# An attention block and a gelu MLP on one core: the second tile's hidden layer in seven half-products, two groups of weight sums exchanged, and a new order of slots

## The chip, the cores and the metric

The kernel runs on one core of one Trainium2 chip. The metric is device time in microseconds of one execution of the whole program. Besides the bare times there is one profiled execution of the kernel, whose trace gives the start and the duration of every instruction. TensorE is called PE, VectorE DVE, ScalarE ACT, GpSimd POOL; SP is the queue that issues almost all DMAs.

## What is computed

A recurrent attention block (RWKV-6 style, batch 4, 8 heads, 768 steps, head size 48), whose output is read as 3072 rows of 384, followed by an MLP with an exact gelu:

```python
for t in range(S):
    cur = einsum('bhd,bhe->bhde', u[None] * k[:, :, t], v[:, :, t])
    y[:, :, t] = einsum('bhd,bhde->bhe', r[:, :, t], state + cur)
    state = w[:, :, t, :, None] * state + einsum('bhd,bhe->bhde', k[:, :, t], v[:, :, t])
x = y.transpose(0, 2, 1, 3).reshape(3072, 384)
h = x @ w_in                      # 384 x 2048
g = 0.5 * h * (1.0 + erf(h / sqrt(2)))
out = g @ w_out                   # 2048 x 384
```

All of it is fp32; the two weights arrive as float64 and are converted on the chip, in sixteen pieces.

## The kernel before

**Tiles and loops.** The 3072 tokens are eight tiles of 384 (`T`), numbered 0 to 7. Loop x of the main loop (from `for x in range(NX)`, L1242) issues three things woven into each other: the MLP of tile x-1 (`mlp`, L916), the attention of tile x (`attention`, L369) from where the loop before left it, and the first steps of the attention of tile x+1. After loop 7 the MLP of tile 7 runs alone. Every engine executes its own instructions strictly in the order in which they are issued, so the weaving fixes, for PE, DVE, ACT and SP, who stands behind whom.

**The order.** It is written out by hand as strings, `PLAN[x]` (L39). Each letter takes one step of a generator: `.` the MLP, `s` the attention of tile x, `f` that of tile x+1, `l` a load of the next tile's r, k, w, v, `c` a step of the weight conversion (loop 1), `w` sums of weights, `x` sums of x. What a string leaves over is drained at the loop's end (all but `f`), and the `s` of the next loop begins where `f` stopped.

**The hidden layer, two ways.** For tile 0 and 1 h is computed plainly: for each of 16 blocks of 128 hidden units, three products with 384 columns (L1070), then gelu on ACT (L1073; for even tiles the last 128 columns apart, L1075). For tiles 2 to 7 `h_halves` (L949) cuts x and w_in into halves and computes a 2 x 2 block product with seven products instead of eight, in products of 192 columns (all at L945): for each q of four, `first` (4 matmul instructions), `second` (8), `third` (8), `fourth` (8), `fifth` (4), `sixth` (4), `seventh` (8), 44 in all. Each plain product is two instructions, too: 96 for a tile. PSUM of `first` is copied to a second bank (L988), `fifth` and `sixth` are copied into g (L1008, L1012), `third` and `seventh` into one of two `o_sb` buffers (L981), which DVE adds to g (L999, L1017).

**The sums that this needs.** `h_sums` (L886, eight steps) makes them of w_in: w(1,0) grows in place by w(1,1), three others go to `s_of`. `sums_of_x` (L907, five steps: t3, t1, t2, t4, l01) makes them of the tile's own x, when its attention is done. `homes` (L873) takes the buffers for both, from those of the conversions. The second layer does the same with `w_sums` (L854, eight steps) and `first_sum` (L863, two): its seven products are run by `product` (L1082) in two halves of 8 instructions (L1084). `of_alone` products (end of the MLP of an even tile, 32 instructions) handle its last 128 tokens; odd tiles end with five more products. For tile 0 the second layer is plain (16 steps, L1164), and its two results are copied by ACT (L1170).

**The attention of a tile** from 2 on runs, in this order: DVE products (`f` steps, L407 stt, L394, L427, L401, L435), a layout by ACT and DVE (L573 to L579), bursts of small products on PE with h=4 and h=16 (L604; three bursts each, in even tiles the last two of h=16 are together with the first), whose results DVE (h=4, L637) or ACT (h=16, L620) copies out and so frees the PSUM pair, two of which exist; DVE updates (L658 to L669); transposes on DVE and twelve small DMAs (L552, L547), ACT's `L711`, the products kv (L727), the chain of states on DVE (L742, 20 of them), the products `inside` (L768) into PSUM pairs that the chain must have freed, a DVE read of their last columns called fence (L780), and the products y (L813) onto the same PSUM, which wait for the fence; then copies and DMAs into xT (L836 to L843). Tile 1 has another first half: six levels of products d (L468), updates (L521), copies (L532, for h=16 and 32 on ACT, L529), and a PE transpose kt (L701) that ACT copies (L703).

**Loop 1 and 2 before.** In loop 1 the letter `w` stands for masks (four steps) and `w_sums`; in loop 2 for `first_sum` and `h_sums`. The conversions are finished in loop 1: ACT makes three passes for each piece (L349 to L352), DVE a shift (L361) and an add (L365).

```python
        fast = x > 1
        if fast:
            yield from h_halves()
```

Of the kernel before, what the change touches and what calls it, by code (L numbers as in the profile page):

```python
# [38 lines left out]
PLAN = {  # L39
    0: ".lls.....sslsc.lsslll.sl.sls..sl.lscsl..sss.lscs.lscs.s.clll.s..s.pcsss...wss..sccs.ffp",  # L40
    1: (
        ".cswc.ccc.cccss.lc.ccscs..cc.cs.cclwcsc.ccssc.c.cccsccc..ssccc.c.lcls.cc.ccsc.w.clwscclccc"
        ".c.swcw.ss.ccs.lcsc..cwcccslccslff..w..fw.wfs..f..flffffffww"
    ),
    2: (
        "...l...s..ws.swssswssss.sslsw...ssss.sssws.ll..ws.w..lw.sw.wl.sls.sls..lf.s....sf..f.f.xx."
        "fxl.x.x"
    ),
    3: (
        "l..sss..s.s..s.s....s...s.ssllss.sss.s.s.ss.l..lsss..ssslss.ss.s..s......s..ls.llssf.sf.sf"  # L50
        "lf.f.x.x..xxfffxf"
    ),
    4: (
        "...s...lsl......s.s....sss..ssss..s..ss..s..s...llssslss....sl.sss...s...sll.sl.s.sfs..fsf"
        ".ff..xl.x.xfffxffx"
    ),
    5: (
        ".l..........ls.ss...s.sslls.ssss..ss.sls...sss..sssssl.ss.s..s.......s.lssll.sfsf.f.s.ff.x"
        "..x.xxxl"
    ),  # L60
    6: (
        "sss.sls.....s......ls.s....s.sssssss..s.....s.ss....s.s.ssss.s.l.ss.l.ls.l...s.l.lslssf.s."
        ".ffs..lff.xx..xffxffx"
    ),
    7: "......s.s....s.s...s.ssssss...sss.ss...sss..ssss.s...ss...s...s.s.ss.s.s.s.x.x...xxx",
}


# [5 lines left out]
def kernel(  # L74
# [6 lines left out]
    w_out: bass.AP,  # L81
    out: bass.AP,
):

    nc = tc.nc  # L100
    NX = rkw.shape[0]
    NP = u.shape[1]
# [22 lines left out]
    def fewer_pairs():  # L125
        pairs_of_banks.close()
        pools["d"] = ctx.enter_context(tc.tile_pool(name="pe", bufs=2, space=PSUM))
        pools["u"] = ctx.enter_context(tc.tile_pool(name="pu", bufs=1, space=PSUM))
        for i in range(2):
            u = bank_u(i)  # L130
            nc.tensor.matmul(u, lhsT=zeros[:, 0:128], rhs=zeros, start=True, stop=True)
# [51 lines left out]
    def load(x, dma):  # L183

        if x >= NX:
            return
        loaded[x] = [None, None]
        for i in (0, 2, 1):
            t = bufs[x % 2 if i == 0 else 1]
            for j in range(3):  # L190
                a = i * ALL + j * ALL // 3
                dma.dma_start(out=t[:, a:a + ALL // 3], in_=rkw[x, :, a:a + ALL // 3])
                yield
        load_v(x, dma)
        yield
# [12 lines left out]
    def weight_in(i, gate=False):  # L208

        if i < len(pieces):  # L210
            dst, src = pieces[i]
            raws[i] = cv.tile([128, PIECE], I64, name="raw", bufs=AHEAD) if wide else None
            if wide:
                dst = raws[i].rearrange("p (a c) -> p a c", a=dst.shape[1])
            if not gate:
                nc.sync.dma_start(out=dst, in_=src)
                return
            for a in range(dst.shape[1]):
                if wide:
                    nc.vector.memset(dst[:, a].bitcast(U32)[:, 0:1], 0)  # L220
                nc.sync.dma_start(out=dst[:, a], in_=src[:, a])
                yield
# [84 lines left out]
    def make_quarter_masks():  # L307
        make_fine()
        yield
        for (h, a), m_q in m_qs.items():  # L310
            nc.vector.tensor_tensor(out=quarter[h][a], in0=s_qs[h][:, 0:m_q.shape[1]], in1=m_q, op=ALU.is_equal)
            yield
# [538 lines left out]
    def w_quarter(b, c, k):  # L851
        return w_out_sb[:, b * HF + k * FG:b * HF + (k + 1) * FG, c * HM:(c + 1) * HM]

    def w_sums():  # L854

        sums.extend(cv.tile([128, HF, HM], F32, name="t", tag="raw", bufs=AHEAD) for _ in range(3))
        for out_, x, y in ((0, (0, 1), (0, 0)), (1, (1, 1), (0, 1)), (0, (1, 1), 0), (2, (1, 0), 0)):
            for k in range(2):
                o = sums[out_][:, k * FG:(k + 1) * FG]
                nc.vector.tensor_sub(o, w_quarter(*x, k), sums[y][:, k * FG:(k + 1) * FG] if isinstance(y, int) else w_quarter(*y, k))  # L860
                yield

    def first_sum():  # L863
        for k in range(2):
            nc.vector.tensor_sub(w_quarter(0, 1, k), w_quarter(0, 1, k), w_quarter(0, 0, k))
            yield
# [6 lines left out]
    def homes():  # L873

        more = [cv.tile([128, PIECE], I64, name="s", tag="raw", bufs=AHEAD).bitcast(F32) for _ in range(2)]
        s3_sb.append(more[0][:, 0:HF * 128].rearrange("p (f c) -> p f c", f=HF))
        x_sums.extend(z[:, i * HT:(i + 1) * HT] for z in (more[0][:, HF * 128:], more[1][:, HF * 128:]) for i in range(2))
        spare = [cv.tile([128, PIECE], F32, name=name) for name in ("f", "f", "e", "e")]
        for i, name in enumerate(("s1", "s2")):
            s12_of[name] = [z[:, 0:FG * 128].rearrange("p (f c) -> p f c", f=FG) for z in spare[2 * i:2 * i + 2]]  # L880
        second = [more[1][:, i * WI:(i + 1) * WI] for i in range(HK)]
        third = [s_home[:, i * WI:(i + 1) * WI] for i in range(HK)]
        fourth = [z[:, FG * 128:] for z in spare]
        s_of.extend((second, third, fourth))

    def h_sums():  # L886

        def w(a, c, k):
            return w_in_sb[:, a * HK + k * 2:a * HK + k * 2 + 2, c, :]

        def pieces_of(i, k):
            return s_of[i - 2][2 * k:2 * k + 2]

        for k in range(2):
            for i in range(2):
                nc.vector.tensor_sub(pieces_of(3, k)[i], w(0, 0, k)[:, i], w(1, 0, k)[:, i])
            yield
            nc.vector.tensor_add(w(1, 0, k), w(1, 0, k), w(1, 1, k))
            yield
            for i in range(2):  # L900
                nc.vector.tensor_sub(pieces_of(2, k)[i], w(1, 0, k)[:, i], w(0, 0, k)[:, i])
            yield
            for i in range(2):
                nc.vector.tensor_sub(pieces_of(4, k)[i], w(0, 1, k)[:, i], pieces_of(2, k)[i])
            yield

    def sums_of_x(x):  # L907

        xT = xT_of[x]
        x00, x01, x10, x11, l0, l1 = (xT[:, c, b * HT:(b + 1) * HT] for c in range(3) for b in range(2))  # L910
        t2, t3, t4, l01 = x_sums
        for o, a, b in ((t3, x11, x01), (x01, x01, x00), (t2, x11, x01), (t4, x10, t2), (l01, l0, l1)):
            nc.vector.tensor_sub(o, a, b)  # L913
            yield

    def mlp(x):  # L916
# [142 lines left out]
            late[:] = [rest]  # L1059

        s1, s2, s3 = [], [], []
        fast = x > 1
        if fast:
            yield from h_halves()
        for n, group in enumerate(() if fast else (0, 2, 1, 3) if halves else range(4)):
# [156 lines left out]
    def prepare_apart():  # L1222
        for i in range(2, 2 + HALFWAY):
            prepare(i)
            yield

    def next_v():
        load_v(1, nc.sync)
        yield

    def warm():
        for _ in range(2):
            keep_warm(3, True)
            yield

    def masks_and_sums():
        yield from make_quarter_masks()
        yield from w_sums()

    pieces_of_w = weights()  # L1240
    slots = iter(())
    for x in range(NX):  # L1242
        if x == 2:
            homes()
        following = attention(x + 1, 0) if x + 1 < NX else iter(())
        if x == 0:
            streams = {
                ".": units[0], "s": units[1], "f": following, "c": pieces_of_w, "w": next_v(), "x": warm(),
                "p": prepare_apart(),
                "l": chain(weight_in(0, True), islice(second, 5), weight_in(1, True), second, weight_in(2, True)),  # L1250
            }
        else:
            streams = {
                ".": mlp(x - 1), "s": slots, "f": following,
                "l": load(x + 1, nc.sync),
                "x": sums_of_x(x) if x > 1 else iter(()),
                "w": masks_and_sums() if x == 1 else chain(first_sum(), h_sums()) if x == 2 else iter(()),
                "c": pieces_of_w if x == 1 else iter(()),
            }
        for c in PLAN[x]:  # L1260
            next(streams[c], None)
        for c in ".slxwp" if x == 0 else ".slxwc":
            while next(streams[c], streams) is not streams:
                pass
        slots = following
        if x == 1:
            fewer_pairs()
    for _ in mlp(NX - 1):
        pass
# [60 lines left out]
```

## Time and profile before

| what | us |
|---|---|
| median of 3 runs (lowest, highest) | 594.47 (593.58, 595.18) |
| span of the profiled execution, first to last instruction | 595.7 |
| PE busy in it | 578.9 (97%) |
| DVE, ACT busy | 440.2 (74%), 280.9 (47%) |
| first product of the MLP of tile 0, 1, 2 | 48.85, 124.43, 197.12 |
| of tile 3, 4, 5, 6, 7 | 261.28, 332.47, 396.74, 467.93, 532.42 |
| last product of all begins | 592.4 |

Times of instructions are counted from the start of the span. A line of a timeline gives the start, the time from the first start to the last end, engine, line, operation, output and inputs with shapes, and how many; in brackets the idle time of the engine before it and what ended it. PE's instructions overlap: sixteen products of 192 columns follow one another every 162 ns, while each is shown with 326 ns, so gaps of PE under some 0.16 us do not show as idle, and the distance between starts is what counts.

### The profile page before, as it was taken

What the parts mean: (1) busy time and instruction counts of PE and PEld (TensorE: products, weight loads), DVE (VectorE), ACT (ScalarE), POOL (GpSimd) and SP (SyncE); (2) the same over time, 40 slices, a digit from 0 to 9 for tenths busy, and PEclk for the clock granted to TensorE, in tenths of its full rate; (3) what the DMA queues carried; (4) which work ended last, traced back from release to release, by engine and by line L of the source; (5) the groups of instructions that cost most, each with busy time, mean ns of one, the idle gap of its engine ahead of it and who ended that gap; (6) DMA issues with size and microseconds to landing.
All of it is one profiled execution on the core that took longest, in us unless ns stands there. A gap on an engine that the chain in (4) does not pass through costs nothing. (4 is left out here: it accounts for less than half of the span.)

```text
span 595.7 us, 17417 instructions
## 1 busy us (share of the span) xinstructions
PE 578.9 (97%) x7536; PEld 513.5 (86%) x7536; DVE 440.2 (74%) x854; ACT 280.9 (47%) x648; POOL 8.0 (1%) x21
## 2 busy tenths in 40 slices
PE   5789999999999999999999999999999999999998
PEld 3566666676799999999999999999999999999997
DVE  5868767888969987687859987688759998521332
ACT  2158889333622358045561458135560465435400
POOL 3100000000000000000000000000000000000000
PEclk9989999999999999999999999999999999999999
DMA  7657671120152211241023411330015200210000
GB/s 235 193 175 273 211 237 61 71 94 1 19 148 79 74 54 24 74 137 36 1 52 90 124 37 18 96 110 11 3 32 161 72 2 5 37 46 0 1 15 33
DMA packets 51004, 46.80 MB, mean 79 GB/s; under 512 B 31728, under 2 KB 36080, under 8 KB 50928
## 3 DMA queue, kind: packets, MB, share of 16 engines
q1 hardware_dynamic: 50832, 45.62, 25.5%
q8 instruction: 59, 0.97, 0.7%
q14 instruction: 17, 0.14, 0.1%
q10 hardware_dynamic: 96, 0.07, 0.1%
HBM read 36.24 MB, written 4.72 MB: 69 GB/s over the span
## 5 line engine op out<-in xcount | busy, mean ns | idle before, releaser
L945 PE MATMUL h_ps<-xT,w_in_sb 128*128 128x192 f32 x480 | 95.4, 330 | 0.5 <-DVE o_sb L1207 0.5
L945 PEld LDWEIGHTS h_ps<-xT,w_in_sb 128*128 128x128 f32 x480 | 79.7, 190 | 3.9 <-ACT g L977 1.5
L1070 PE MATMUL h_ps<-xT,w_in_sb 128*128 128x384 f32 x192 | 64.5, 491 | 0.9 <-ACT rkw L1075 0.9
L1070 PEld LDWEIGHTS h_ps<-xT,w_in_sb 128*128 128x128 f32 x192 | 35.7, 190 | 25.5 <-ACT rkw L1075 1.7
L1084 PE MATMUL o_ps<-w_out_sb,g 128*128 128x192 f32 x224 | 39.7, 326 | 0.0
L1084 PEld LDWEIGHTS o_ps<-w_out_sb,g 128*128 128x128 f32 x224 | 37.0, 190 | 0.3
L945 PE MATMUL u_ps<-s,w_in_sb 128*128 128x192 f32 x192 | 35.3, 327 | 0.0
L468 PEld LDWEIGHTS d<-rkw 64*64 64x64 f32 x1152 | 20.8, 147 | 16.7 <-issue 11.9
L620 ACT COPY a_sb<-d 32x256 f32<-32x256 f32 (+8 forms) x90 | 32.6, 362 | 4.6 <-PE d L604 3.1
L945 PEld LDWEIGHTS u_ps<-s,w_in_sb 128*128 128x128 f32 x192 | 31.8, 190 | 0.2
L1084 PE MATMUL o_ps<-w_out_sb,f 128*128 128x192 f32 x176 | 31.6, 329 | 0.0
L1084 PE MATMUL o_ps<-t,g 128*128 128x192 f32 x176 | 31.4, 329 | 0.0
L1084 PE MATMUL o_ps<-w_out_sb,e 128*128 128x192 f32 x176 | 31.4, 329 | 0.0
L1084 PE MATMUL o_ps<-t,e 128*128 128x192 f32 x176 | 31.2, 328 | 0.0
L1084 PE MATMUL o_ps<-t,s 128*128 128x192 f32 x176 | 30.9, 327 | 0.0
L468 PE MATMUL d<-rkw 64*64 64x64 f32 (+1 forms) x1152 | 23.5, 235 | 7.2 <-DMA rkw<-in_rkw_dram 4.1
L742 DVE SCALAR_TENSOR_TENSOR st<-st,tot_sb,kv_ps 128x48 f32<-128x48 f32 x160 | 29.0, 256 | 1.7 <-PE kv_ps L727 1.6
L637 DVE COPY_PREDICATED a_sb<-quarter,d 128x480 f32<-128x480 uint8 (+5 forms) x54 | 23.2, 438 | 8.6 <-PE d L604 7.3
L1084 PEld LDWEIGHTS o_ps<-t,g 128*128 128x128 f32 x176 | 28.7, 190 | 0.4
L1084 PEld LDWEIGHTS o_ps<-w_out_sb,e 128*128 128x128 f32 x176 | 28.7, 190 | 0.3
L1084 PEld LDWEIGHTS o_ps<-w_out_sb,f 128*128 128x128 f32 x176 | 28.7, 190 | 0.3
L1084 PEld LDWEIGHTS o_ps<-t,e 128*128 128x128 f32 x176 | 28.8, 190 | 0.2
(163 smaller groups left out, 1127.0 us busy)
## 6 DMA issues: line engine op xcount, KB each, us to landing
rkw<-in_rkw_dram SPq DMA_DIRECT2D x54, 256.0 KB, 4.0
raw<-in_w_out_dram SPq DMA_DIRECT2D x8, 768.0 KB, 4.5
v_in<-in_v_dram SPq DMA_DIRECT2D x8, 584.0 KB, 3.9
raw<-in_w_in_dram SPq DMA_DIRECT2D x5, 768.0 KB, 6.5
out_dram<-o_sb SPq DMA_DIRECT2D x20, 192.0 KB, 2.0
rkw<-kx SPq DMA_DIRECT2D x72, 48.0 KB, 2.0
rkw<-in_rkw_dram SPq DMA_DIRECT2D x6, 384.0 KB, 6.8
raw<-in_w_in_dram SPq DMA_DIRECT2D x9, 256.0 KB, 4.7
```

The lines of the kernel that those rows point to most:

```text
L468: nc.tensor.matmul(d[half[p], g, n * width:(n + 1) * width], lhsT=kc[half[g], b, i, p], rhs=right(half[g], b, i, p), start=True, stop=True)
L620: nc.scalar.copy(out=at[z, g, first:behind, (a + 1) * h:], in_=d[z, :, :, to] if g == slice(None) else d[z, :, to])
L637: nc.vector.copy_predicated(out=an[:, :, :, :, (a + 1) * h:], mask=mask.to_broadcast(data.shape), data=data)
L742: nc.vector.scalar_tensor_tensor(out=stq[:, q, c], in0=stq[:, q, c - 1] if c else b4[:, q, NC - 1], scalar=totq[:, q, c:c + 1], in1=kvs[q ...
L945: nc.tensor.matmul(o, lhsT=lhsT, rhs=rhs, start=start, stop=True, skip_group_check=True)
L1070: nc.tensor.matmul(h_ps, lhsT=w_in_sb[:, f // FI, j, f % FI * 128:(f % FI + 1) * 128], rhs=xT[:, j, :], start=(j == 0), stop=(j == NJ - 1))
L1084: nc.tensor.matmul(o, lhsT=lhs(j), rhs=rhs(j), start=start and j == 0, stop=(j == HF - 1), skip_group_check=True)
```

## The change

The MLP of tile 1 takes the half-products too (`fast = x > 0`). So `h_sums`, with `homes` in front of it, moves into loop 1, behind the masks, and `w_sums` moves from loop 1 into loop 2, ahead of `first_sum`; `sums_of_x` is issued in loop 1 as well. The strings of loops 1 to 7 are new; that of loop 0 is the same. Blank lines at the head of the function go, which moves later line numbers up by 16; this document uses those of the kernel before until the result.

```diff
     1: (
-        ".cswc.ccc.cccss.lc.ccscs..cc.cs.cclwcsc.ccssc.c.cccsccc..ssccc.c.lcls.cc.ccsc.w.clwscclccc"
-        ".c.swcw.ss.ccs.lcsc..cwcccslccslff..w..fw.wfs..f..flffffffww"
+        "c.ccc.c.cslcc.c..cccs.ccs.cs.slcccscc.c.ccccsl.cwscc.cccc.cscsscccls..ccsc..ccscc.cslcscwc"
+        "sl..wcssc..ccwcwlwcws..c.ccsww.wsllsf.....ffxff..fl.f.xwxfwxx"
     ),
     2: (
-        "...l...s..ws.swssswssss.sslsw...ssss.sssws.ll..ws.w..lw.sw.wl.sls.sls..lf.s....sf..f.f.xx."
-        "fxl.x.x"
+        "swlws......s.l..s...w.s..w..wsswsw.l.ssswsl...sw.l..sw.ss..s..s..ssslss.s.s.....s...ss..sl"
+        "slslf.sf.sf.f..f.xx.lxxx"
     ),
     3: (
-        "l..sss..s.s..s.s....s...s.ssllss.sss.s.s.ss.l..lsss..ssslss.ss.s..s......s..ls.llssf.sf.sf"
-        "lf.f.x.x..xxfffxf"
+        "..ssss...ssl.ll......sls...s.ssss.s..lsss.s.ss...sss.ssssss..s..s.....ls..s.ssl.lsslsf.f.."
+        "f.x.xlx.f.xx"
     ),
     4: (
-        "...s...lsl......s.s....sss..ssss..s..ss..s..s...llssslss....sl.sss...s...sll.sl.s.sfs..fsf"
-        ".ff..xl.x.xfffxffx"
+        "ssssl..l..ls.s....ss....s....s..ssssls..s..sssls.s.....s.s.ss..ss..s.s..ls.s..s.sssl.llf.."
+        "s.fsf..flfx..x.xxx"
     ),
     5: (
-        ".l..........ls.ss...s.sslls.ssss..ss.sls...sss..sssssl.ss.s..s.......s.lssll.sfsf.f.s.ff.x"
-        "..x.xxxl"
+        "s...s.s..s.....ssl.ss.l..s.ssss.lss..sss.ss....sss.sssss...s..l..ss..l..ss.lss.sslllsf.f.."
+        "f..xl.xff.xxfx"
     ),
     6: (
-        "sss.sls.....s......ls.s....s.sssssss..s.....s.ss....s.s.ssss.s.l.ss.l.ls.l...s.l.lslssf.s."
-        ".ffs..lff.xx..xffxffx"
+        "s...lss...s....s..ss.l...sss..ss.sl.sss.s....l.ss...sl.s.ss..sss.ss...l.s...s..slsls.lfsf."
+        ".fs..ff.xlx..xxx"
     ),
-    7: "......s.s....s.s...s.ssssss...sss.ss...sss..ssss.s...ss...s...s.s.ss.s.s.s.x.x...xxx",
+    7: "sssss....s........ss...s.sss.ssss..ss...s.s.sss.ssss.s......ss.s..s.s..sssss....x.x.x.xx",
...
-        fast = x > 1
+        fast = x > 0
...
     def masks_and_sums():
         yield from make_quarter_masks()
-        yield from w_sums()
+        homes()
+        yield from h_sums()
...
     for x in range(NX):
-        if x == 2:
-            homes()
...
-                "x": sums_of_x(x) if x > 1 else iter(()),
-                "w": masks_and_sums() if x == 1 else chain(first_sum(), h_sums()) if x == 2 else iter(()),
+                "x": sums_of_x(x),
+                "w": masks_and_sums() if x == 1 else chain(w_sums(), first_sum()) if x == 2 else iter(()),
```

Read letter by letter, the strings differ in this: loop 1 takes 8 steps of the next attention instead of 12, loops 3 to 6 take 4, 5, 6 and 5 instead of 9, 10, 5 and 9; in loops 1, 3, 5 and 7 no `.` stands any more between `inside` and y (before: five in loop 1, one, two and one in the others).

## The prediction

> **What bounds the kernel now.** I read the table of engines first, then the busy tenths by slice, then busy time by stretch.
>
> ```profile
> PE 578.9 (97%) x7536; PEld 513.5 (86%) x7536; DVE 440.2 (74%) x854; ACT 280.9 (47%) x648; POOL 8.0 (1%) x21
> ...
> PE   5789999999999999999999999999999999999998
> ...
> DVE  5868767888969987687859987688759998521332
> ```
>
> PE is the bound: after the first three slices it never stops, and 11.6 of its 16.8 idle us lie before 48.85, where nothing changes. So a product less is time less, and a wait added to PE is time added. DVE's 9s (slices 14 to 16, 20, 21) show where a second bound is near: the stretches of loop 2.
>
> ```profile
> 124.60:160.80 36.20, 36.20 (x320) 22.38 (x320) 33.65 (x48) 14.15 (x33) 0.00 (x0) 1.00 0.11 36
> 160.80:197.00 36.20, 36.20 (x465) 35.24 (x464) 29.72 (x74) 10.50 (x30) 0.00 (x0) 1.00 0.36 100
> ```
>
> Columns: stretch, length, then busy us of PE, its weight loads, DVE, ACT, POOL, granted clock. PE is full, the clock is 1.00, DVE has 63.4 of 72.4 us, ACT 24.7.
>
> **1. What is removed from PE.** From the timeline of PE:
>
> ```profile
> 124.43 15.64 PE L1070 MATMUL h_ps<-xT,w_in_sb 128*128 128x384 f32 x48
> ...
> 160.90 2.76 PE L1084 MATMUL o_ps<-w_out_sb,g 128*128 128x192 f32 x16
> 163.50 2.76 PE L1084 MATMUL o_ps<-t,g 128*128 128x192 f32 x16
> ```
>
> 48 instructions of 384 columns take 140.01-124.43 = 15.58 us from start to start, 0.3247 each; 16 of 192 take 2.60, 0.1625 each. Tile 1's 96 plain ones cost 31.2 us, the 4 x 44 = 176 new ones 28.6: **-2.6**. The products of tiles 2 to 7 already run at this distance, so the price is seen, not guessed; ends -2.8 and -2.3.
>
> [...]
>
> Each time small products interrupt large ones, PE loses about 0.14 (24 of L1070 take 63.13 to 71.06, 7.93, against 24 x 0.3247 = 7.79). In loops 1, 3, 5 and 7 the new strings put `inside` and y side by side, one interruption less each: 4 x 0.14 = **-0.6** (ends -0.6, 0).
>
> **2. What lies beside other work.** Tile 1's h now has 20 copies on ACT (L988, L1008, L1012, L981, 0.47 each or 0.39 from start to start): 8 us on an ACT busy 24.7 of 72.4, hidden. The eight DVE adds (L999, L1017, 0.46 apart, 3.7 us), `w_sums` in place of `h_sums` (8 x 0.87 = 7.0 for 5.7), the five x sums (0.3 each) and four `f` steps that loop 1 no longer takes (0.9+0.4+1.3+2.4 = 5) go to DVE in loops 1 and 2. DMAs are the same in number; SP's order moves little against what waits for it. So much costs nothing as long as DVE is ahead of PE when PE asks; where it isn't, see 4.
>
> **3. Loop 1.** Read along the new string, with the before's clock for what is equal. (a) The first products d (diag) come after the third h block instead of the first, so the third block meets the gelu of the first, which ACT did at 53.69 to 54.13 behind a conversion: a wait of about 1.3 in place of the 0.88 now idle at 57.53, **+0.4** (0 to 0.8). (b) y follows `inside` at once, so PE waits for the fence, and DVE has the chain and three steps of `h_sums` ahead of the fence. PE: at the end of level h=16 both orders are alike (89.6); then o 11 steps x 1.30, small groups 1.54+1.30+1.54+1.56, interruptions 0.7, and (a): 111. DVE: ACT is free for the last conversions at about 89.4; 4 conversion passes of 2.82, the copies 1.85, 1.55 and 1.45 give 105.5; then the last add 0.87, the chain 3.5, the three steps 2.0, fence 0.3: 112.2; PE may go 0.16 later. **+1.4** (0.4 to 2.5). Today the fence (110.62) is 6.5 us early. (c) The two plain results of tile 0 are copied by ACT (L1170, 116.60 and 117.25, to 117.73), and the next product needs the second bank. Today PE does y meanwhile:
>
> ```profile
> 110.49 6.72 PE L1164 MATMUL o_ps<-w_out_sb,g 128*128 128x384 f32 x20
> 117.14 1.63 PE L813 MATMUL y_ps<-rkw,st 64*64 64x64 f32 x96
> 118.70 5.47 PE L1084 MATMUL o_ps<-w_out_sb,rkw 128*128 128x192 f32 x32
> ```
>
> With y gone from there PE would be ready at 117.14 and the bank at 117.89: **+0.75** (0.4 to 1.1).
>
> **4. Loop 2 and the start of loop 3.** DVE's own work in loop 2 is 63.4 less 12.2 (loop 1's work, done until 136.76) = 51; by part 2 it becomes 51 - 5.7 + 7.0 + 5 + 3.7 = 61, and some 4 come over from loop 1 (behind the fence DVE has 17.4 us of it left and waits 0.6 for xT's DMAs, PE 14: y 1.56, five o steps 6.5, 0.75, 5.2): 65 of 70, 93%, and it must also wait for PE's results. The two places at the end meet it: between kv and y PE has 3 halves, `inside`, one half and interruptions = 7.0, DVE chain 4.0, stt 3.0, u2 and fence 0.5 = 7.5: **+0.5** (0 to 1.5). And `fifth` of tile 2 wants the second x sum 0.65 us after the loop begins, as tile 6's did at 469.29, where PE stood 0.54: **+0.6** (0 to 1.5).
>
> **5. Loops 3 to 7, where only the order is new.** Four kinds of place, each with its row.
>
> ```profile
> 521.21 1.63 PE L768 MATMUL y_ps<-a_sb,v_in 64*64 64x64 f32 x96
> 522.76 1.57 PE L1084 MATMUL o_ps<-w_out_sb,e 128*128 128x192 f32 x8
> ...
> 522.91 0.16 DVE L780 COPY fence<-y_ps 128x2 f32<-128x2 f32 x1 [0.45 <-PE y_ps L768]
> ```
>
> Loop 7: `inside` is over at 522.76, the fence ends at 523.07. A product follows what frees it by 0.16 (below), so y beside it would start at 523.23: 0.47, in loops 3, 5 and 7 **+1.4** (0.9 to 1.8).
>
> ```profile
> 382.42 1.46 PE L1084 MATMUL o_ps<-t,s 128*128 128x192 f32 x8
> 384.22 1.63 PE L768 MATMUL y_ps<-a_sb,v_in 64*64 64x64 f32 x96 [0.33 <-DVE st L742]
> ```
>
> Loop 5: only two halves stand between kv and `inside`, and PE waits for the chain; without it `inside` would start at 382.42+1.30+0.14 = 383.86, so 0.36. (The chain ends at 384.42, the first pair is free two instructions earlier, 384.06: hence the 0.16.) Loops 3 and 7 had four and three halves and get two, too: **+0.7** (0.2 to 1.2).
>
> ```profile
> 223.71 2.04 PE L604 MATMUL d<-kx,rkw 64*64 64x96 f32 x80
> ```
>
> Loop 3: ACT copies the first burst of h=16 from 224.83 for 2.59 (L620), so its pair is free at 227.58, 3.87 after the bursts began. The third burst needs it. Today `sixth` and `fourth` stand between (it starts at 227.83); in loops 3, 5 and 7 now only `fourth`: 1.97+1.30+0.14 = 3.41. 3 x 0.46 = **+1.4** (0.6 to 1.8).
>
> ```profile
> 304.03 2.27 ACT L620 COPY a_sb<-d 32x256 f32<-32x256 f32 x6
> 306.31 3.28 ACT L620 COPY a_sb<-u_ps 32x128 f32<-32x128 f32 x12
> ```
>
> Loop 4: these copies and L711 (2.09) run on ACT between results of the second layer; kv needs L711. In loop 4 the second group now stands behind the copy of the fifth product (5.2+0.44 after the third's): 5.64+3.27+2.09+0.16 = 11.1, PE 8 x 1.30 = 10.4. In loops 5 and 7 copies 4.2, L711 2.1, two small ones 0.5 = 6.9 against five halves, 6.5. **+1.4** (0 to 2.4). Loops 2 and 6 have a half or more of room.
>
> **The sum.** -2.6 -0.6 +0.4 +1.4 +0.75 +0.5 +0.6 +1.4 +0.7 +1.4 +1.4 = +5.35. The profiled span, 595.7, is 1.2 above the median of the bare runs, which leaves nothing for what lies around it; the difference is added to the median, 594.47: **599.8**.
>
> **Rivals.**
> *ACT is earlier than I count.* 3b, the third burst and kv (1.4+1.4+1.4) hang on ACT's queue, in loops 1, 3, 4, 5 and 7. If ACT takes its copies 0.5 us earlier in each, as its 53% idle time might allow, they vanish: 595.6, not slower than can be told; with 0.3 they are halved. Against it: the copies cannot start before the bursts end. Chance 0.12.
> *All waits are covered.* If ACT and DVE are everywhere done before PE asks, only part 1 stays, 594.5-3.2 = 591.3. Against it: at the four fences nothing lies between the two products, however early the engines are. 0.06.
> *DVE is the bound of loop 2.* The 65 of 70 us are 5 short of full; if its waits for PE (6 us today after 167) remain, DVE is behind all through tile 1's h, its adds free the two `o_sb` buffers late, and PE stops at L981: up to 4 more, 603.8. It decides from a lag of some 6 us, a quarter of the h, on; it is 4 at the start by my count. 0.14.
> *Weight loads set the pace of tile 1's narrow products.* Each has a load of 0.190 us; end to end 176 of them are 33.4, +2.2 in place of -2.6: 604.6. Against it: loads overlap in every other tile (distance 0.1625). [...] 0.02.
> My forecast: 0.66.
>
> **Numbers.** Low 594.5 takes in the first rival and the low ends together (waits of 3.3); high 603.5 most of the third. Within 0.3% (1.8 us, about what a measurement can tell) lies the first rival and the lower edge of the forecast: 0.13. Faster: 0.07. Slower: 0.80.
>
> **What would show it.** Right: L945 in tile 1 takes 28.6 us from first to last; PE idle by the wait list at L813 in four loops, before L604's third burst, at L727; L780 in loop 1 after three L896/L898/L904 instructions. Wrong: loops 3, 5 and 7 last no longer than 64.2, 64.3 and 64.5; or PE stands in tile 1's h behind L981.

## The result and the profile after

| what | before | after | ratio, 95% interval |
|---|---|---|---|
| median, us (runs) | 594.83 (4) | 602.83 (4: 599.58 to 603.37) | 1.0131 [1.0094, 1.0168] |
| once more, beside other kernels | 593.91 (17) | 600.42 (4: 599.75 to 601.79) | 1.0111 [1.0096, 1.0125] |

The change costs 6.5 to 8.0 us; 5.35 were forecast. There are two traces of the changed kernel, of executions of 603.07 us (span 601.3) and 599.75 us (span 598.0). The spans differ mostly ahead of tile 0's MLP, which begins at 47.27 and 45.01. What can be compared is the time from its first product to the start of the last product of all: 543.6 us before, 550.8 and 549.7 after. From here on, line numbers are those of the changed kernel (before's less 16) unless a before-based kernel is named; a loop's length is counted between the first products of two MLPs.

| loop | 1 | 2 | 3 | 4 | 5 | 6 | 7 | rest |
|---|---|---|---|---|---|---|---|---|
| before | 75.6 | 72.7 | 64.2 | 71.2 | 64.3 | 71.2 | 64.5 | 60.0 |
| after | 78.0 | 72.2 | 66.8 | 71.6 | 65.1 | 71.3 | 65.8 | 60.0 |
| after, 2nd trace | 77.2 | 71.9 | 67.1 | 71.6 | 65.1 | 71.3 | 65.5 | 60.0 |

The table of engines, then busy time by stretch (columns as in the prediction):

```profile
PE 576.1 (96%) x7616; PEld 523.8 (87%) x7616; DVE 444.8 (74%) x867; ACT 288.4 (48%) x668; POOL 8.0 (1%) x21
```
```profile
125.22:161.00 35.78, 34.49 (x319) 33.28 (x318) 34.53 (x55) 18.05 (x41) 0.00 (x0) 1.00 0.15 48
161.00:197.40 36.40, 36.40 (x548) 35.15 (x547) 29.84 (x68) 14.80 (x43) 0.00 (x0) 1.00 0.23 60
```

PE is busy 2.8 us less than before although it has 80 products more: that is the saving. Its idle time went from 16.8 to 25.2 us: that is the loss, and more. DVE is busy 34.53 of the first 35.78 us of loop 2, 96%. Where PE stands, loop 1 and the start of tile 1:

```profile
107.98 1.78 PE L752 MATMUL y_ps<-a_sb,v_in 64*64 64x64 f32 x96
111.23 1.68 PE L797 MATMUL y_ps<-rkw,st 64*64 64x64 f32 x96 [1.47 <-DVE fence L764]
112.84 6.72 PE L1148 MATMUL o_ps<-w_out_sb,g 128*128 128x384 f32 x20
119.48 5.47 PE L1068 MATMUL o_ps<-w_out_sb,rkw 128*128 128x192 f32 x32
...
127.33 2.22 PE L929 MATMUL h_ps<-xT,w_in_sb 128*128 128x192 f32 x12 [1.29 <-DVE xT L897]
```
```profile
105.45 3.58 DVE L726 SCALAR_TENSOR_TENSOR st<-st,tot_sb,kv_ps 128x48 f32<-128x48 f32 x20
108.95 0.76 DVE L888 TENSOR_TENSOR f<-w_in_sb,s 128x256 f32<-128x256 f32 x2
109.62 0.76 DVE L880 TENSOR_TENSOR s_home<-w_in_sb 128x256 f32<-128x256 f32 x2
110.42 0.69 DVE L882 TENSOR_TENSOR w_in_sb<-w_in_sb 128x512 f32<-128x512 f32 x1
111.02 0.22 DVE L764 COPY fence<-y_ps 128x2 f32<-128x2 f32 x2
```

The second fence shows what 3b of the prediction said: the chain, then three sums of w_in, then the fence, and PE behind it. L1068 starts 0.41 us after the last L1148, where 0.32 is usual, and 0.1 us ahead of the second copy of the plain results (ACT, 119.60): it does not wait for that one. Tile 1's `fifth` waits for its second x sum (126.92), which stands on DVE behind 7.5 us of work, most of it four first steps of the next attention. Loop 3, loop 7 and kv of loop 5:

```profile
229.40 0.56 PE L588 MATMUL d<-kx,rkw 64*64 64x96 f32 x16 [0.39 <-ACT a_sb L604]
...
250.43 1.63 PE L752 MATMUL y_ps<-a_sb,v_in 64*64 64x64 f32 x96 [0.33 <-DVE st L726]
252.35 1.16 PE L797 MATMUL y_ps<-rkw,st 64*64 64x64 f32 x64 [0.17 <-DVE fence L764]
254.37 0.68 PE L797 MATMUL y_ps<-rkw,st 64*64 64x64 f32 x28 [0.86 <-issue]
...
383.58 1.59 PE L711 MATMUL kv_ps<-v_in,rkw 64*64 64x48 f32 x90 [0.15 <-ACT rkw L695]
...
528.92 1.46 PE L1068 MATMUL o_ps<-t,s 128*128 128x192 f32 x8 [0.75 <-issue]
```

Bracketed idle times understate a wait, since shown ends overlap; waits below are the distance between starts above the usual one. (A change from large products to small ones has 0.09 us above it even without a wait, in the kernel before as well.) The lines marked "issue" have no releaser and were foreseen by nobody: 1.07 us within y of loop 3, 0.96 right behind y of loop 7.

### The profile page after: what moved, and what is told of

It is laid out like the page before. It is cut to its first block, busy times and chain, and to the rows that moved or that the text cites. A ratio compares the mean times of both kernels' runs of the same rounds, so it can differ in the third digit from the quotient of the medians.

```text
span 601.3 us, 17626 instructions
## 1 busy us (share of the span) xinstructions
PE 576.1 (96%) x7616; PEld 523.8 (87%) x7616; DVE 444.8 (74%) x867; ACT 288.4 (48%) x668; POOL 8.0 (1%) x21
## 4 chain that ended last, share of the span: by engine, by line
PE 79%; ACT 9%; DVE 6%; issue 4%; DMA 2%; ACTq 0%; SPq 0%; DVEq 0%
PE o_ps L1068 28%; PE h_ps L929 18%; PE u_ps L929 14%; PE d L588 4%; PE h_ps L1054 3%; ACT a_sb L604 3%; PE d L452 3%; PE y_ps L797 2%; DVE st L726 2%; PE y_ps L752 2%; PE kv_ps L711 2%; DMA rkw<-in_rkw_dram 2%; ACT e L334 1%; ACT f L333 1%; PE o_ps L1148 1%
## 5 line engine op out<-in xcount | busy, mean ns | idle before, releaser
L929 PE MATMUL h_ps<-xT,w_in_sb 128*128 128x192 f32 x560 | 111.3, 330 | 2.2 <-DVE xT L897 1.3
L929 PEld LDWEIGHTS h_ps<-xT,w_in_sb 128*128 128x128 f32 x560 | 93.1, 190 | 6.2 <-DVE xT L897 1.6
L929 PE MATMUL u_ps<-s,w_in_sb 128*128 128x192 f32 x224 | 41.5, 329 | 0.0
L1068 PE MATMUL o_ps<-w_out_sb,g 128*128 128x192 f32 x224 | 39.8, 326 | 0.0
L929 PEld LDWEIGHTS u_ps<-s,w_in_sb 128*128 128x128 f32 x224 | 36.9, 190 | 0.6
L1068 PEld LDWEIGHTS o_ps<-w_out_sb,g 128*128 128x128 f32 x224 | 37.0, 190 | 0.0
L1054 PE MATMUL h_ps<-xT,w_in_sb 128*128 128x384 f32 x96 | 32.6, 493 | 1.8 <-ACT rkw L1059 1.4
L1068 PE MATMUL o_ps<-w_out_sb,f 128*128 128x192 f32 x176 | 32.2, 331 | 0.0
L1068 PE MATMUL o_ps<-t,s 128*128 128x192 f32 x176 | 31.1, 328 | 0.8 <-issue 0.8
L726 DVE SCALAR_TENSOR_TENSOR st<-st,tot_sb,kv_ps 128x48 f32<-128x48 f32 x160 | 29.1, 260 | 3.4 <-PE kv_ps L711 3.3
L1068 PE MATMUL o_ps<-t,g 128*128 128x192 f32 x176 | 31.4, 330 | 0.0
L1068 PE MATMUL o_ps<-t,e 128*128 128x192 f32 x176 | 30.7, 327 | 0.0
L1068 PE MATMUL o_ps<-w_out_sb,e 128*128 128x192 f32 x176 | 30.4, 326 | 0.0
L983 DVE TENSOR_TENSOR g<-g,o_sb 128x384 f32<-128x384 f32 x28 | 15.3, 546 | 20.3 <-ACT o_sb L965 20.3
L1054 PEld LDWEIGHTS h_ps<-xT,w_in_sb 128*128 128x128 f32 x96 | 17.8, 190 | 14.2 <-ACT rkw L1059 2.0
L1068 PEld LDWEIGHTS o_ps<-t,s 128*128 128x128 f32 x176 | 28.9, 190 | 0.8 <-issue 0.6
L1068 PEld LDWEIGHTS o_ps<-t,g 128*128 128x128 f32 x176 | 28.6, 190 | 0.5
L1068 PEld LDWEIGHTS o_ps<-w_out_sb,f 128*128 128x128 f32 x176 | 28.6, 190 | 0.5
L1068 PEld LDWEIGHTS o_ps<-t,e 128*128 128x128 f32 x176 | 28.9, 190 | 0.1
L1068 PEld LDWEIGHTS o_ps<-w_out_sb,e 128*128 128x128 f32 x176 | 28.9, 190 | 0.0
```

The costliest lines, as they stand in the source:

```text
L726: nc.vector.scalar_tensor_tensor(out=stq[:, q, c], in0=stq[:, q, c - 1] if c else b4[:, q, NC - 1], scalar=totq[:, q, c:c + 1], in1=kvs[q ...
L929: nc.tensor.matmul(o, lhsT=lhsT, rhs=rhs, start=start, stop=True, skip_group_check=True)
L983: nc.vector.tensor_add(g_of(q, 0, 1), g_of(q, 0, 1), z)
L1054: nc.tensor.matmul(h_ps, lhsT=w_in_sb[:, f // FI, j, f % FI * 128:(f % FI + 1) * 128], rhs=xT[:, j, :], start=(j == 0), stop=(j == NJ - 1))
L1068: nc.tensor.matmul(o, lhsT=lhs(j), rhs=rhs(j), start=start and j == 0, stop=(j == HF - 1), skip_group_check=True)
```

## Experiments

All ratios are to runs of the kernel before on the same chip. A diff stands against the kernel that the text names, or else against the changed one; `...` marks what is left out of it. Below each expectation stand the ratio, its 95% interval and the difference of the medians.

**1. The changed kernel again.**

> The changed kernel once more, unaltered, for a tighter ratio and a second trace. Its trace has two idle stretches of PE of about 1 us inside or right behind the products y of loops 3 and 7 (253.29 and 527.95) for which the trace names no releaser, and a 16 KB packet of instructions in flight just before each. Theory: instructions come late where `inside` and y, 192 short products, stand side by side, so both stretches return at the same instructions. Rival: chance of one execution; then they are gone or elsewhere. Time by both: 1.010 to 1.016 of before.

1.0111 [1.0096, 1.0125]. Both stretches return at the same products (loop 3: behind the same one of y's, 1.34 us; loop 7: in front of the same L1068, 0.63 us). So they belong to the kernel, not to one execution.

**2. and 3. The change in two halves.** First only the strings of loops 3 to 7 on the code of before, then the rest of the change with before's strings for loops 3 to 7.

```diff
     3: (
-        "l..sss..s.s..s.s....s...s.ssllss.sss.s.s.ss.l..lsss..ssslss.ss.s..s......s..ls.llssf.sf.sf"
+        "..ssss...ssl.ll......sls...s.ssss.s..lsss.s.ss...sss.ssssss..s..s.....ls..s.ssl.lsslsf.f.."
...
```

> The code and the strings of loops 0 to 2 are those of before; only the strings of loops 3 to 7 are the new ones. Theory: most of the loss is their waits (third burst at ACT, y at the fence, kv at ACT, `inside` at the chain), whatever tile 1 does: the lengths of loops 3 to 7 in the two traces differ by 2.63+0.42+0.84+0.09+1.34 = 5.3, so +4 to +5.5 us. Rival: what makes these loops late is DVE, held up by its extra work of loops 1 and 2; then the new strings alone cost 0 to 1 us.

1.0090 [1.0065, 1.0114], +4.9 us: the theory. Its trace has the waits of the changed kernel in these loops (third burst 3 x 0.56, fence 3 x 0.38, kv 0.44, 0.37 and 0.37 us), but only one stretch named "issue", 1.13 us within y of loop 7.

> The other half: the new code and the new strings of loops 1 and 2, with the strings of loops 3 to 7 of before. Theory: +1.4 to +2.5 us, the sum of loops 1 and 2 in the traces (+1.95 and -0.51) and of tile 2's start (1.04). Rival, DVE held up by the extra work: +5 us and more, the waits of loops 3 and 4 among it.

1.0042 [1.0025, 1.0059], +2.3 us. (Loop 1 is 2.37 and 1.59 us longer than before's in the two traces, not the 1.95 of the expectation.) The halves add up within the intervals (4.9 + 2.3 = 7.2; the whole, beside them: 6.5). So about two thirds of the loss is the order of loops 3 to 7 by itself; it needs none of DVE's extra work of tile 1. That the sum fits so well is partly chance: in the trace of the second half, loops 1 to 3 are only 1.6 us longer than before's, and loops 6 and 7, whose strings are before's, 1.4 us. The reason in loop 6 stands below experiment 7.

**4. Tile 1 with a mended loop 1**, and with before's strings of loops 3 to 7 as in experiment 3.

```diff
-        "c.ccc.c.cslcc.c..cccs.ccs.cs.slcccscc.c.ccccsl.cwscc.cccc.cscsscccls..ccsc..ccscc.cslcscwc"
-        "sl..wcssc..ccwcwlwcws..c.ccsww.wsllsf.....ffxff..fl.f.xwxfwxx"
+        "c.sccc.c.clcc.c..cccs.ccs.cs.slcccscc.c.ccccsl.cwscc.cccc.cscsscccls..ccsc..ccscc.cslcscwc"
+        "sl..wcssc..ccwcwlwcws..c.ccs..sll.swwwf...ffff.xx.lxxx..fffww"
...
-        "slslf.sf.sf.f..f.xx.lxxx"
+        "slslf.sf.sf.f...xx.lxxxf"
```

> As the run before, but loop 1 is mended where its trace shows PE waiting: the first products d stand before the third h block, seven steps of the second layer stand between `inside` and y with the sums of w_in behind the fence, and the x sums of tiles 1 and 2 are issued earlier. Theory: the seven products pay for tile 1 too, 176 x 0.1625 for 96 x 0.3247 us, -2.6, once the waits of 1.55, 1.68, 1.46 and 1.04 us go: -3.5 to -1.0 us against before. Rival: the new work of DVE (adds, sums) costs PE as much as the products save, in other places: 0 to +2 us.

1.0041 [1.0025, 1.0057], +2.8 us: the rival's side, and above its +2. Loop 1 is indeed 0.7 us shorter than before's (74.9), without a wait at the fence. But DVE now does the sums and the first steps of tile 2 later, and PE waits for what follows from them: 0.58, 0.90 and 0.72 us in loop 2, which is 0.4 us longer than before's, and 0.77 and 1.18 us in loop 3, which is 1.9 us longer. Those of loop 2:

```profile
130.00:140.00 10.00, 8.84 (x88) 8.28 (x90) 9.90 (x15) 6.25 (x15) 0.00 (x0) 1.00 0.26 80
140.00:150.00 10.00, 9.45 (x144) 8.94 (x136) 9.90 (x15) 4.55 (x11) 0.00 (x0) 1.00 0.01 2
```
```profile
132.97 0.59 PE L929 MATMUL h_ps<-xT,f 128*128 128x192 f32 x2 [0.42 <-ACT g L992]
...
139.18 1.88 PE L588 MATMUL d<-kx,rkw 64*64 64x96 f32 x80 [0.74 <-ACT g L992]
...
143.76 0.65 PE L579 MATMUL d<-rkw 64*64 64x48 f32 x32 [0.55 <-DVE a_sb L621]
```

DVE is the third of the busy times: 9.9 of 10 us. The named ACT copies (L992) stand in ACT's queue behind a gelu that waits for an add of DVE (132.02) and a layout that waits for DVE's products (136.19).

**5. The x sums earlier.**

```diff
-        "sl..wcssc..ccwcwlwcws..c.ccsww.wsllsf.....ffxff..fl.f.xwxfwxx"
+        "sl..wcssc..ccwcwlwcws..c.ccsww.wsllsf.....ffxfxf..fl..xfxxfww"
...
-        "slslf.sf.sf.f..f.xx.lxxx"
+        "slslf.sf.sf.f...xx.lxxxf"
```

> The changed kernel with the x sums of tiles 1 and 2 taken earlier among the steps of the next attention (loops 1 and 2), so that the `fifth` products of tiles 1 and 2 need not wait (1.15 to 1.46 and 1.04 us in the two traces of the changed kernel). Theory A: the waits are a matter of order alone and go: 2.3 us less than the changed kernel, +4.3 us against before. Theory B: DVE is full from the end of loop 1 on, so what is put behind the x sums (the next attention's first steps) is late by as much, and PE waits for its bursts in loops 2 and 3, as it did in the run with the mended loop 1 (4.4 us of such waits in its trace): +6 to +8 us.

1.0152 [1.0126, 1.0177], +8.4 us, a little above B. Both `fifth` waits are gone and loop 2 is 1.0 us shorter than in the second trace of the changed kernel; in loop 3 PE stands 1.95 us for a copy queued behind a gelu that waits for an add of DVE, and the two traces are equally long (549.7). The wait changed its name only. (The traced execution, 599.48 us, is the fastest of the five; the others, up to 604.67, have no trace.)

**6. The sums of w_out later**, on top of experiment 4.

```diff
-        "swlws......s.l..s...w.s..w..wsswsw.l.ssswsl...sw.l..sw.ss..s..s..ssslss.s.s.....s...ss..sl"
-        "slslf.sf.sf.f...xx.lxxxf"
+        "sls......s.l..s....s....sss.l.ssssl.w.ww.sw.wl.w.s.sws..sw..wws..ssslss.s.s.....s...ss..sl"
+        "slslf.sf.sf.f..f.xx.lxxx"
```

> The kernel with the mended loop 1 and the old strings of loops 3 to 7 once more; in loop 2 the eight sums of w_out (7.0 us of DVE) now stand behind the bursts of h=4 instead of ahead of them, and the x sums of tile 2 where the changed kernel has them. In the mended kernel DVE was busy 39.9 of the 41 us from 108 to 149, and PE waited 0.58, 0.90 and 0.72 us in it and 0.78 and 1.18 at the start of loop 3. If DVE's order is what counts, these go, one wait of 1.04 at tile 2's `fifth` comes: its products end 3 us earlier than the mended kernel's, -1 to +0.5 us against before. If DVE is full whatever stands first, the second layer's products of tile 1 wait for the sums at 160 and later: +1.5 to +3 us.

1.0118 [1.0098, 1.0138], +6.5 us: worse than either. The early waits vanish, later ones come, and loop 2 takes 77.0 us. To the two waits shown come two of kv, 1.15 and 0.60 us, and right behind them 3.41 us at a granted clock of 0.5:

```profile
155.69 1.54 PE L1068 MATMUL o_ps<-t,g 128*128 128x192 f32 x8 [0.39 <-DVE t L844]
...
159.80 0.89 PE L588 MATMUL d<-kx,rkw 64*64 64x96 f32 x32 [1.76 <-DVE a_sb L671]
```

**7. Experiment 4 with the x sums of tile 2 put back** and two sums of w_out one place later.

```diff
-        "swlws......s.l..s...w.s..w..wsswsw.l.ssswsl...sw.l..sw.ss..s..s..ssslss.s.s.....s...ss..sl"
-        "slslf.sf.sf.f...xx.lxxxf"
+        "swlws......s.l..s...w.s..w..wsssww.l.ssswsl...sw.l..sw.ss..s..s..ssslss.s.s.....s...ss..sl"
+        "slslf.sf.sf.f..f.xx.lxxx"
```

> The kernel with the mended loop 1 and the old strings of loops 3 to 7 a third time; in loop 2 the x sums stand where the changed kernel has them, and two of the sums of w_out one place later, behind the copies of the first burst. From the traces: loop 1 as in the mended kernels, 74.9 to 75.0 us; loop 2 their 73.13 less the wait of 0.72 before the third burst, 72.4; loop 3 as in the run that had the same end of loop 2, 64.9: together 212.3 against 212.4 us before, so 0 us (-1 to +1) against before. Then the seven products of tile 1 can at best be had without loss, the 2.6 us saved going to waits for DVE. Rival: as in the last two runs, what is moved comes back as a wait elsewhere: +2 us or more.

1.0029 [1.0008, 1.0050], +1.5 us, above the +1 of the expectation: the lowest of the kernels with tile 1 in halves, and still slower than before. In its trace loop 1 has a wait of 1.19 us for the transfers of tile 0's xT (48.59), in place of before's 1.04 at 57.53; loop 2 takes 73.0 and loop 3 64.8 us, 0.3 and 0.7 more than before's.

In experiments 3, 4 and 7 a part of the loss lies where neither DVE's extra work nor a new string is: at y's fence in loop 6, 1.02, 1.08 and 0.67 us, where before has no wait. There DVE's first step of tile 7, ahead of the fence, starts 61.1, 61.2 and 60.9 us into the loop (before: 59.8), after 1.99, 2.05 and 1.64 us of idle time that a DMA ends (before: 0.73 us). In experiments 6 and 9, with the same string, it starts at 60.1 and 59.8, and the fence costs nothing. DVE and PE of experiment 3:

```profile
456.19 3.01 DVE L391 SCALAR_TENSOR_TENSOR kx<-rkw,u_sb 128x384 f32<-128x384 f32 x4 [1.99 <-DMA out_dram<-o_sb]
```
```profile
459.27 1.41 PE L797 MATMUL y_ps<-rkw,st 64*64 64x64 f32 x80 [0.86 <-DVE fence L764]
```

Why these transfers land later in some runs than in others stays open.

**8. and 9. Weight sums on GpSimd**, first those of w_out in the changed kernel, then both groups in experiment 4's order (with the changed kernel's string for loop 2; the operations of `h_sums` are moved in the same way as the one shown).

```diff
-                nc.vector.tensor_sub(o, w_quarter(*x, k), sums[y][:, k * FG:(k + 1) * FG] if isinstance(y, int) else w_quarter(*y, k))
+                nc.gpsimd.tensor_sub(o, w_quarter(*x, k), sums[y][:, k * FG:(k + 1) * FG] if isinstance(y, int) else w_quarter(*y, k))
```

> The changed kernel with the eight sums of w_out (loop 2, 8 x 0.87 = 7.0 us of DVE) on GpSimd, which is idle there (busy 8.0 us in the whole span). If DVE is full in loop 2 and this is why tile 2's x sums come late, the wait of 1.04 us there goes and loop 2 gets shorter where PE waits for DVE: 1 to 1.5 us less than the changed kernel, +5 to +5.6 against before. Rival 1: these sums fill gaps of DVE in which it waits for PE, so nothing changes: +6.6. Rival 2: GpSimd at work slows DVE down: +7 and more.

> The kernel with the mended loop 1 and the old strings of loops 3 to 7, and both groups of weight sums (w_in and w_out, 12.7 us of DVE) on GpSimd; the string of loop 2 is that of the changed kernel. In the mended kernel PE's waits for DVE and for ACT behind DVE in loops 2 and 3 came to 4.4 us, and its products ended 3.0 us later than before's. If DVE's extra work is what eats the gain of the seven products, they go and the gain shows: -2 to 0 us against before. Rival: GpSimd is too slow for the sums of w_in, which have 20 us between the last conversion and tile 1's first products; then PE waits at the start of tile 1: +2 us or more.

1.0244 [1.0223, 1.0265], +13.9 us, and 1.0196 [1.0171, 1.0221], +11.0 us: in the first rival 2, by far more than I had put; in the second the start of tile 1 as the rival said, but for another reason. GpSimd's queue is empty, so its sums start as soon as the conversions allow, at the end of loop 1, beside the sums of w_in and the first steps that DVE has ahead of what PE waits for, and these take two to five times as long. From the first of the two kernels, DVE and GpSimd:

```profile
109.74 2.47 DVE L888 TENSOR_TENSOR f<-w_in_sb,s 128x256 f32<-128x256 f32 x2
112.13 3.96 DVE L880 TENSOR_TENSOR s_home<-w_in_sb 128x256 f32<-128x256 f32 x2
```
```profile
108.17 7.63 POOL L844 TENSOR_TENSOR t<-w_out_sb,t 128x768 f32<-128x768 f32 x4
```

The same two DVE lines took 0.76 each above. Two steps of L880 in 3.96 us are one for each step of GpSimd (7.63 / 4 = 1.91). Not all of DVE's work is held up: beside GpSimd the chain (L726) takes its usual 3.58 us in the first kernel, and a transpose (L378) its usual 1.78 in the second. What sets these two apart from the ones held up, no run shows. PE stood 6.6 us at loop 1's fence in the first kernel, and 9.27 us at tile 1's `fifth` in the second, whose sums of w_in were done at 110.85: there too it was DVE, held up by the sums of w_out (its first step of tile 2, L391, takes 6.60 us instead of 3.07). Each of these two waits goes with 6.83 us at a granted clock of 0.5, which adds to the loss.

**10. A half between `inside` and y.**

```diff
-        "sl..wcssc..ccwcwlwcws..c.ccsww.wsllsf.....ffxff..fl.f.xwxfwxx"
+        "sl..wcssc..ccwcwlwcws..c.ccsww.wsll.sf....ffxff..fl.f.xwxfwxx"
...
-        "s...s.s..s.....ssl.ss.l..s.ssss.lss..sss.ss....sss.sssss...s..l..ss..l..ss.lss.sslllsf.f.."
+        "s...s.s..s.....ssl.ss.l..s.ssss.lss..sss.ss....sss.sssss...s..l..ss..l..ss.lss.sslllf.sf.."
...
```

> The changed kernel with one letter moved in loops 1, 3, 5 and 7: one step of the second layer (8 products, 1.30 us) stands between `inside` and y. The changed kernel stood +6.6 us above before in the run beside this. Of its waits those at the four fences go (3 x 0.38, and 1.3 of loop 1's 1.68), four interruptions of 0.14 come back. Theory for the two idle stretches of loops 3 and 7 with no releaser (1.34 and 0.63 in that trace, 1.07 and 0.96 in the first): PE runs out of instructions, because `inside` and y side by side use up 192 products and 192 weight loads in 3.1 us; in three traces such a stretch ends 1.25 to 1.45 us after the end of a 16 KB packet of instructions. Then they go as well, and the run is 2.4 - 0.6 + 2.0 = 3.8 us shorter: +2.8 us against before. Rival: they are tied to the place in the code, not to the density of instructions; then they stay, +4.8 us.

1.0167 [1.0143, 1.0192], +9.4 us: as a total, both theories missed. In its own places the step did what it should: no wait is left at any of the four fences, and no "issue" stretch in loop 3 or 7, whose lengths are 65.6 and 65.0 (second trace of the changed kernel: 67.1 and 65.5). The loss is in loop 2 (73.4 for 71.9) and in loop 6 (76.8 for 71.3), at the `fifth` of tiles 1 and 5, and the trace shows what y's early place was good for. SP at the end of loop 5, of this kernel and of the changed one (second trace):

```profile
391.42 0.34 SPq L913 DMA_DIRECT2D out_dram<-o_sb  x1
391.81 4.75 SPq L827 DMA_DIRECT2D xT<-ysb  x6
```
```profile
389.29 3.72 SPq L827 DMA_DIRECT2D xT<-ysb  x6
```

y is later by 1.3 us, so a store of the second layer gets in front of its six transfers on SP; these begin 2.5 us later, take 1.0 us longer, and end 3.55 us later (396.56 for 393.01). DVE waits for xT (2.65 us idle at 397.43), and PE for DVE, 2.97 us at tile 5's `fifth`. Then the clock falls. Busy time by stretch, of this kernel and of the changed one:

```profile
400.00:410.00 10.00, 8.49 (x34) 8.49 (x35) 8.54 (x12) 2.39 (x5) 0.00 (x0) 0.66 0.32 103
```
```profile
400.00:410.00 10.00, 10.00 (x62) 9.77 (x62) 9.93 (x14) 5.38 (x13) 0.00 (x0) 1.00 0.24 79
```

The number behind ACT's and POOL's busy times is the granted clock, 0.66 for 1.00: in the same 10 us PE does 34 products for 62.

**11. Room for ACT's copies.** The third bursts one half later in loops 3, 5 and 7, other copies earlier.

```diff
-        "..ssss...ssl.ll......sls...s.ssss.s..lsss.s.ss...sss.ssssss..s..s.....ls..s.ssl.lsslsf.f.."
+        "..ssss...ssl.ll......sls...s.ssss.s..lsss.s.ss...sss..ssssss.s..s.....ls..s.ssl.lsslsf.f.."
...
-    7: "sssss....s........ss...s.sss.ssss..ss...s.s.sss.ssss.s......ss.s..s.s..sssss....x.x.x.xx",
+    7: "sssss....s........ss...s.sss.ssss..ss...s.s.sss..sssss.ss..s......s.s..sssss....x.x.x.xx",
```

> The changed kernel with the third burst of h=16 one half-product later in loops 3, 5 and 7, and the copies of the other bursts one to two steps earlier in ACT's order in loops 4, 5 and 7, so that L695 is done when kv asks. The waits there are 3 x 0.56 and 0.47 + 0.36 + 0.39 = 2.9 us in the second trace of the changed kernel. If these are single waits, the run is 2.9 us below the changed kernel (1.011 and 1.013 of before so far, +6.6 to +7.8 us): +3.7 to +4.9 us against before. Rival: each is only the first of a row, and what stands behind it (DVE's updates, the next wait at `inside`) takes its place: +5.6 us or more.

1.0176 [1.0150, 1.0203], +9.7 us: the rival. The waits for ACT are gone everywhere; in loop 4, where nothing else moved, that is 0.6 us of gain (71.0 for 71.6). In loops 3, 5 and 7 the twelve small transfers behind the third burst became later, too, and kv waits for them, 1.30, 1.55 and 0.60 us. In loops 3 and 7 the trace puts these waits down to "issue", but kv's product goes on 0.09 us after one of the transfers has landed. In loop 5, where 3.41 us at a clock of 0.5 come on top:

```profile
383.47 0.28 PE L711 MATMUL kv_ps<-v_in,rkw 64*64 64x48 f32 x2 [1.34 <-DMA rkw<-kx]
384.12 2.17 PE L711 MATMUL kv_ps<-v_in,rkw 64*64 64x48 f32 x89 [0.37 <-DMA rkw<-kx]
```

**12. Before, with y beside `inside` in loops 2 to 7.**

```diff
-    7: "......s.s....s.s...s.ssssss...sss.ss...sss..ssss.s...ss...s...s.s.ss.s.s.s.x.x...xxx",
+    7: "......s.s....s.s...s.ssssss...sss.ss...sss..ssss.s...ss...s...s.s.ss.s.ss..x.x...xxx",
...
```

> The kernel before, whose tile 1 is plain, with only y moved up to stand beside `inside` in loops 2 to 7. Theory: each of the six fences then costs PE 0.38 us and saves an interruption of 0.14, +1.4 us; tile 6's wait for its x sum (0.71) goes, since x is ready earlier; and PE runs short of instructions in some of the six places, about 1 us each, of which the packets of instructions in flight decide: +1 to +4 us in all, with idle stretches of PE that have no releaser in or right behind y, 1.2 to 1.5 us after the end of a 16 KB packet. Rival: these stretches belong to the changed code; then +0.7 us.

1.0209 [1.0178, 1.0240], +12.0 us, far outside both. No stretch without a releaser came at y. In loops 2 to 6 of this order a step of the next attention (before's L407, 3.04 us on DVE) stands between the chain and the fence, so the fences cost 2.22, 0.97, 1.36, 1.82 and 1.90 us; only loop 7, which has no next tile, shows the 0.38. Behind the first of them the clock is 0.5 for 3.41 us. In loop 5:

```profile
388.08 1.63 PE L768 MATMUL y_ps<-a_sb,v_in 64*64 64x64 f32 x96 [0.33 <-DVE st L742]
391.32 1.64 PE L813 MATMUL y_ps<-rkw,st 64*64 64x64 f32 x96 [1.61 <-DVE fence L780]
```

## Why the prediction was right, and where it was short

Direction and cause held: the products saved are given back by waits that the new places cause. The size was 1.2 to 2.7 us short. Term by term, us, first and second trace of the changed kernel, each against the trace of before:

| term | forecast | measured |
|---|---|---|
| tile 1's products | -2.6 | -2.2 (distances from each product of h to PE's next one: 31.55 in all before; 29.3 after, waits taken off) |
| interruptions | -0.6 | -0.9 (45 changes from large products to small for 49, 0.09 each, and 0.14 for each change back) |
| (a) third h block | +0.4 | +0.5, -0.3 (1.55, 0.75 against 1.04) |
| (b) fence of loop 1 | +1.4 | +1.68 in both |
| (c) copies of the plain results | +0.75 | +0.1 |
| y of loop 2 | +0.5 | 0 to 0.1 |
| `fifth` of tile 2 | +0.6 | +1.04 in both |
| fences of loops 3, 5, 7 | +1.4 | 3 x 0.38 = +1.14 |
| `inside` of loops 3, 7 | +0.7 | +0.76, +0.75 (0.09 of each interruption taken off) |
| third bursts | +1.4 | 3 x 0.47 = +1.4 (0.56, less the same 0.09) |
| kv of loops 4, 5, 7 | +1.4 | +1.19, +1.22 |
| not in the sum: `fifth` of tile 1 | | +1.46, +1.15 |
| "issue" in loops 3, 7 | | +2.03, +1.97 |
| tile 6's `fifth` no longer waits | | -0.71 |
| `inside` of loops 4 to 6, shorter waits | | -0.47, -0.44 |

The terms of the sum come to +4.8 and +4.0 instead of +5.35, those that were not in it to +2.3 and +2.0; together that is the 7.2 and 6.1 us of the traces within 0.2. So the shortfall is what the sum left out. That the terms in it came near their total is partly luck: (c) and y of loop 2 were 1.1 us too high, the products, loop 1's fence and tile 2's `fifth` 1.1 us too low.

The step that failed is part 2's sentence that the added DVE work costs nothing "as long as DVE is ahead of PE when PE asks". I priced the second x sum of tile 2, but not that of tile 1, which has the same place in the code and stands behind four `f` steps in the new string. (c) failed because I took the next product to need the second bank; it follows the first copy (118.95 and 0.48 long) at 119.48. A misreading did no harm: the 9s in DVE's line of tenths stand in slices 11, 13, 14, 22, 23 and 31 to 33, the first three of them in loop 2 and at its end. And the price of an interruption, 0.14, was read where large products change to small ones only; with the change back it is 0.23.

The two largest waits that I could not have read from before are the "issue" stretches. What the runs show: at y there are eleven in six traces (both of the changed kernel, experiments 2, 5, 8 and 11). In each the product that ends the stretch waits for no semaphore (kv in experiment 11 does), and PE resumes 1.2 to 1.5 us after the end of a packet of the queue that the profile calls instruction (60 packets of 16 KB for 15,232 products and weight loads, 254 each); with the changed code they stand at the same products each time. `inside` and y together are 384 instructions in 3.1 us. With a half in between, or with a longer wait at the fence (experiment 12), they are absent. But they are absent in loop 5, too, where the changed kernel has the two side by side with a fence of 0.38, in experiment 2's loop 3, and in experiment 12's loop 7: side by side is not enough. That PE had used up what was loaded, so that it matters when a packet ends, is the reading that fits all of this; no run changed the loading itself, so it stays a reading.

The rival "DVE is the bound of loop 2" had 0.14 and the wrong form: DVE never stops tile 1's products at L965's buffers. In the form in which it is true, DVE is nearly full in the first half of loop 2 (34.53 of 35.78 us), and experiments 4, 6 and 7, with before's order of loops 3 to 7, show three ways to spread the waits, none of which ends below before. There the 2.2 us of tile 1 went into waits for DVE in loops 2 and 3 (4.2 us of them in experiment 4) and into loop 6's fence, where DVE in its turn waits for a transfer. Without the wait at that fence experiment 7 would still be some 0.8 us above before (an estimate: 1.5 less 0.67). Nor did the narrow products come out dear, as the rival of the weight loads had it: tile 1's median distance is 0.163 us at 192 columns, with loads of 0.190, against 0.323 at 384.

What stays open: the single causes in loops 3 to 7 were not taken away one at a time without another coming up; their sum is shown by experiment 2, their names are read from the traces. A version that beats before was not found.

## What to carry to other kernels

Before spending a saving of the bounding engine, read the engine that has to feed it in that very stretch: at 96% busy, work added there was paid for in each of the three orders tried. When a product is moved, follow both ends of it: the wait that it now meets (the fence) and the deadline that it now keeps or misses (y, six transfers, the x sum, `fifth`). A wait that vanishes in the trace is a gain only if the next one behind it was late by less.

## What the runs showed of the hardware

In six traces a wait of PE cost more than its length. From within waits of 2.97, 6.6 and 9.27 us (experiments 10, 8 and 9) the granted clock was 0.5 for 6.83 us; behind one of 2.22 (12) and behind two close ones of 1.55 and 0.58 (11) and of 1.15 and 0.60 (6) it was 0.5 for 3.41. Behind others it stayed at 1.00, up to the 2.69 us at tile 1's `fifth` in experiment 10. Such stretches of 3.41 us also lie ahead of tile 0's MLP, two in the first trace of the changed kernel and none in the second, whose MLP begins 2.26 us earlier. So the length of a wait alone does not decide: behind 2.22 us the clock fell, behind 2.69 it did not. What does decide, no run shows.

Up to where the strings of loop 1 part, PE's first 1096 products, ACT's first 54 instructions and SP's first 35 transfers start in the same order in the trace of before and in the first of the changed kernel, though the starts of one and the same lie up to 2.7 us apart. So do DVE's first 111, but for a memset of one element (L163) and the instruction beside it, whose starts, 0.08 and 0.01 us apart, stand once in one order and once in the other.
